# A two-level Strassen MLP: weight sums in place, input sums spread over the first block, sums written in PSUM

## The chip, the cores and the metric

The kernel runs on one core of one Trainium2 chip. The metric is the device time of one execution in microseconds; lower is better. Traces are hardware profiles of one execution.

## The reference

```python
x = attention(q, k, v)          # local band + pooled, (2, 8, 576, 64) -> x of 1152 tokens x 512
h = x @ w_in;  g = where(h > 0, h, exp(min(h, 0)) - 1);  x = g @ w_out      # first MLP, d_ff 2048
p = domain_probs / domain_probs.sum(-1)                                   # second MLP: 4 experts
for e in range(4):
    h = maximum(x @ w1[e], 0)                  # 512 -> 1024
    out += p[:, e:e+1] * (h @ w2[e])           # 1024 -> 512
```

The whole is in float32. The change is in the second MLP alone.

## The kernel before, in words

**Precision.** Each fp32 operand is kept as a high part (a ScalarE copy that rounds to fp32r) and a low part (the rest, by a subtraction), and each product is three matmul passes: high x high, low x high, high x low (`mm3`, line 237; `PASSES`).

**Blocks.** The second MLP has 8 blocks (`sbs`): 4 experts by 2 halves of 512 hidden columns. A block multiplies the input (512 x 1152, feature by token) by a 512 x 512 piece of `w1`, takes the relu into `hs` as high and low parts, and multiplies that by 512 rows of `w2` in nine tiles of 128 tokens (`l2e`, four quarters each, psZ), which VectorE scales by the probability and adds into `oacc`.

**Strassen.** The first product uses a 2 x 2 Winograd form, seven products instead of eight. Block 0 (`quad`, four times: `pair` of token quarters by `j`) uses one level: ScalarE copies the first product out of PSUM, VectorE adds the next ones to running sums c1, u2, u3, c22 in `cA` or `cB`; each of four results gets its relu high part (`hi`, ScalarE) and low part (`lo`, VectorE). Blocks 1 to 7 use two levels for three of the seven products (parts 0, 1, 3; `inner`, psA, psB, psC) and one level for the other four (`ready`, psE; `last`, psF and psG). The inner level needs sums of the inputs, which `fold(p)` makes once for all blocks: per part two VectorE sums of 576 columns (high + low), four subtractions of 288, then four high parts on ScalarE (`cp`, line 1034) and four low parts, the first on VectorE and three on GpSimd (line 1134). They go to `xq`, the fourth over an input that block 0 no longer reads (`xin`). Before the change the three folds run one after another when the four quads are issued, with three tile quarters after each.

**Weights of the next block** (`w1_two`). F loads 512 x 512 floats into a slot of the pool `s8` (eight slots of 8 KB a partition; a slot goes back by `done`). On GpSimd, T makes the sums for the inner parts, and S(j) four weight sums for the other products into a buffer `st`. H and HS write high parts on ScalarE, L and LS low parts on GpSimd. F2, H2, L2 do the same for `w2` without sums. An inner part holds a slot as `wq`, the weight sums of one j one as `ws`, the second weights two as `wr`.

**Order.** The program order of every engine is written out by the generators: `weave` takes one step of two generators in turn by a pattern; a step adds its length (0.4 per inner product, 0.8 per product, 0.68 per tile quarter) to a plan clock, and before each step `step` runs every entry of `due` whose time has come. An entry that takes a slot (F, H of the first half, HS, F2, H2) holds up those behind it until a slot is free. `plan` (line 1277) enters the weight steps for the next block relative to its start. An engine works through its own queue in this order and waits there for what an instruction needs. A block starts with `last`, woven with the tiles; the inner products come from plan time 20.0, the first of `ready` at 35.9, and a block is 45.7 long. In the first block the quads end at 27.8.

**PSUM** has eight banks, which `bank` hands out in order of their return (`psb_.done`).

Of the kernel before, what the change touches and what calls it, by code (L numbers as in the profile page):

```python
# [151 lines left out]
def attn_moe_kernel(  # L152
# [12 lines left out]
    nc = tc.nc  # L165
# [778 lines left out]
    def w1_two(n, st_pool):  # L944
# [9 lines left out]
        def F():  # L954
            raw.append(s8.tile([P, KD, SB], F32, name="raw1", uses=7))
            nc.sync.dma_start(raw[0], w1[e, :, c:c + SB].rearrange("(k p) f -> p k f", p=P))
# [4 lines left out]
        def sums(st, a11, a12, a21, a22):  # L961
            tt(out=st[0], in0=a21, in1=a22, op=add)
            tt(out=st[1], in0=st[0], in1=a11, op=sub)
            tt(out=st[2], in0=a11, in1=a21, op=sub)
            tt(out=st[3], in0=a12, in1=st[1], op=sub)
            s8.done(raw[0])
# [35 lines left out]
        def S(j):  # L1002
            sts[j] = st = st_pool[0].tile([P, 4, 2, P], F32, tag="st", name="st")
            x = view()[:, :, :, j]
            sums([st[:, o] for o in range(4)], x[:, 0, :, 0], x[:, 1, :, 0], x[:, 0, :, 1], x[:, 1, :, 1])

        def HS(j):
            mine["s", j] = s8.tile([P, 4, 2, 2, P], F32R, name="ws", uses=2)
            nc.scalar.activation(mine["s", j][:, :, 0], sts[j], AF.Copy)  # L1009

        def LS(j):
            w = mine["s", j]
            tt(out=w[:, :, 1], in0=sts[j], in1=w[:, :, 0].bitcast(F32), op=sub)  # L1013
# [3 lines left out]
    with ExitStack() as ph2:  # L1017
# [30 lines left out]

        def quad(n, j, pair):
# [3 lines left out]
            u = (cA, cB)[j]  # L1053
            c1, u2, u3, c22 = (u[:, i] for i in range(4))
            t = 2 * pair

            def prod(w, x):
                return product(bank("psH", uses=0)[:, :HB], w, x)

            cp(c1, prod(wa[:, 0], xb_[:, 0]))  # L1060
            yield 0.8
            add(u2, c1, prod(ws[:, 1], xt[:, 1]))
            yield 0.8
            add(u3, u2, prod(ws[:, 2], xt[:, 2]))
            yield 0.8
            p5 = prod(ws[:, 0], xt[:, 0])
            add(c22, u3, p5)
            add(u2, u2, p5)
            hi(dest(j, 1, t + 1), c22)
            yield 0.8  # L1070
            add(c1, c1, prod(wa[:, 1], xb_[:, 1]))
            lo(dest(j, 1, t + 1), c22)
            hi(dest(j, 0, t), c1)
            yield 0.8
            add(u3, u3, prod(wa[:, 2], xt[:, 3]))
            lo(dest(j, 0, t), c1)
            hi(dest(j, 1, t), u3)
            yield 0.8
            add(u2, u2, prod(ws[:, 3], xb_[:, 2]))
            lo(dest(j, 1, t), u3)  # L1080
            hi(dest(j, 0, t + 1), u2)
            lo(dest(j, 0, t + 1), u2)
            s8.done(wa)
            s8.done(ws)
            yield 0.8
# [33 lines left out]
        def fold(p):  # L1119

            buf = cB if p == 1 else cC
            f = buf.rearrange("p (a k) b -> p a k b", a=2)
            for pair in range(2):
                x = (xbo, xbo, None, xto)[p][pair][:, p]
                nc.vector.tensor_tensor(  # L1125
                    out=f[:, pair], in0=x[:, 0].bitcast(F32), in1=x[:, 1].bitcast(F32), op=add_
                )
            f11, f21, f12, f22 = (f[:, a, k] for a in range(2) for k in range(2))
            for o, x, y in ((f11, f12, f11), (f12, f22, f12), (f22, f22, f11), (f21, f21, f22)):
                nc.vector.tensor_tensor(out=o, in0=x, in1=y, op=sub)  # L1130
            for k, t in ((0, f11), (1, f22), (2, f12), (3, f21)):
                h, l = xin(p, k)
                cp(h, t)
                (nc.gpsimd if k else nc.vector).tensor_tensor(out=l, in0=t, in1=h.bitcast(F32), op=sub)

# [38 lines left out]

        def ready(n):
# [3 lines left out]
            for pair in range(2):  # L1179
                for j in range(2):  # L1180
                    q_ = 2 * j + pair
                    e[q_] = bank("psE")
                    ps = product(e[q_][:, :HB], wm[n][0]["s", j][:, 1], xto[pair][:, 1])
                    add(cC[:, q_], cC[:, q_], ps)
                    yield 0.8
            for pair in range(2):
                for j in range(2):
                    q_ = 2 * j + pair
                    ps = product(e[q_][:, :HB], wm[n][0]["s", j][:, 0], xto[pair][:, 0], False)
# [3 lines left out]

        late = []

        def flush(k=0):

            while len(late) > k:
                d, c, ps = late.pop(0)
                lo(d, c)  # L1200
                if ps is not None:
                    psb_.done(ps)

        def last(n, pair):
# [10 lines left out]
            for j in range(2):  # L1215
# [3 lines left out]
                ps = product(f[:, :HB], w[:, 3], xbo[pair][:, 2])  # L1219
# [71 lines left out]
        for n in range(4):  # L1291
# [70 lines left out]
```

## Time and profile before

| | |
|---|---|
| median of 3 runs | 692.0 us (690.98 to 701.45) |
| the profiled execution | 692.68 us, its span 690.9 us |
| TensorE busy, mean granted clock | 652.3 us (94%), 0.98 |
| VectorE, ScalarE, GpSimd busy | 473.6, 302.7, 323.8 us |
| HBM | 43.55 MB read, 2.36 MB written |

The span is from the first to the last instruction. The first MLP's products end at about 289 us of the span, the four quads at 318.8, block 1 begins at 362.5, block 2 at 405.7, and the last tile ends the span. [...] PE is TensorE, PEld its weight loads, DVE VectorE, ACT ScalarE, POOL GpSimd, SP the queue that issues all DMAs. "idle before <-releaser" names what ended an engine's wait. Line 240 is the one line of all matmuls, 1031 that of VectorE's sums, 1034 that of ScalarE's copies, 1037 and 1040 relu high and low parts.

### The profile page before, as it was taken

The numbers are of one execution on the slowest core, as the hardware profiler recorded it, in microseconds if no ns is written. First come the engines' busy times: TensorE is split into PE (matmuls) and PEld (weight loads), VectorE is DVE, ScalarE is ACT, GpSimd is POOL, SyncE is SP. The second block draws the span as 40 slices with busy tenths as digits, with TensorE's granted clock in tenths as the row PEclk, the third lists the DMA queues.
The fourth block names the chain that finished last, engine by engine and source line by source line (L and its number), as shares of the span: only waits on it lengthen the run. The fifth ranks groups of instructions, "written<-read, shape, count | busy, mean of one in ns | idle before, by whom it ended". The sixth has DMA issues, their size and how long they took to land.

```text
span 690.9 us, 12309 instructions
## 1 busy us (share of the span) xinstructions
PE 652.3 (94%) x4774; PEld 596.5 (86%) x4774; DVE 473.6 (69%) x976; ACT 302.7 (44%) x820; POOL 323.8 (47%) x304
## 2 busy tenths in 40 slices
PE   8999899989999999999399998998998998998997
PEld 5789789989999999998388987987987987988986
DVE  4899999645678874899757565565565575565652
ACT  4899587435664656443224323223234142233110
POOL 5533322303233537368755847637538458366000
PEclk8999999998999999999799999999999999999999
DMA  9998630051131300100031112101101101110012
GB/s 240 199 213 177 155 89 4 2 184 62 62 122 62 123 1 1 60 3 0 1 122 33 33 58 61 62 1 62 62 0 62 62 1 60 62 62 1 0 46 91
DMA packets 40735, 46.68 MB, mean 68 GB/s; under 512 B 23014, under 2 KB 23014, under 8 KB 40678
## 3 DMA queue, kind: packets, MB, share of 16 engines
q1 hardware_dynamic: 40678, 45.91, 23.8%
q8 instruction: 37, 0.61, 0.4%
q14 instruction: 20, 0.16, 0.1%
HBM read 43.55 MB, written 2.36 MB: 66 GB/s over the span
## 4 chain that ended last, share of the span: by engine, by line
PE 73%; DVE 11%; POOL 6%; ACT 4%; DMA 3%; issue 2%; SPq 0%; ACTq 0%; DVEq 0%
PE psZ L240 24%; PE psH L240 14%; PE psY L240 11%; PE psE L240 6%; PE psA L240 5%; POOL wq L998 4%; PE psB L240 2%; PE psG L240 2%; PE psF L240 2%; PE psS L582 1%; DMA raw<-in_k_dram 1%; DMA raw<-in_moe_w_in_dram 1%; DVE c L1125 1%; DVE w L308 1%; DVE c L1130 1%
## 5 line engine op out<-in xcount | busy, mean ns | idle before, releaser
L240 PE MATMUL psZ<-wr,h 128*128 128x512 f32 x864 | 226.6, 395 | 0.0
L240 PEld LDWEIGHTS psZ<-wr,h 128*128 128x128 f32 x864 | 154.7, 189 | 23.2
L240 PE MATMUL psH<-x,w 128*128 128x288 f32 x768 | 111.1, 301 | 7.5 <-DVE gf L811 4.1
L240 PEld LDWEIGHTS psH<-x,w 128*128 128x128 f32 x768 | 105.9, 192 | 9.3 <-DVE gf L811 4.5
L240 PE MATMUL psY<-g,w 128*128 128x288 f32 x768 | 106.4, 296 | 0.1
L240 PEld LDWEIGHTS psY<-g,w 128*128 128x128 f32 x768 | 103.5, 189 | 0.6 <-DVE g L823 0.3
L1103 DVE SCALAR_TENSOR_TENSOR oacc<-psZ,pn,oacc 128x512 f32<-128x512 f32 x63 | 47.2, 749 | 44.4 <-PE psZ L240 44.4
L1037 ACT ACTIVATE h<-psF 128x288 fp32r<-128x288 f32 x28 | 11.6, 413 | 116.0 <-DVE psF L1031 116.0
L823 POOL TENSOR_TENSOR g<-gf,g 128x288 fp32r<-128x288 f32 x25 | 22.0, 882 | 86.0 <-ACT g L818 84.9
L998 POOL TENSOR_TENSOR wq<-raw,wq 128x512 fp32r<-128x512 f32 x21 | 27.5, 1310 | 50.9 <-ACT wq L994 50.9
L240 PEld LDWEIGHTS psE<-xt,ws 128*128 128x128 f32 x336 | 48.2, 188 | 3.0
L1031 DVE TENSOR_TENSOR c<-psE,c 128x288 f32<-128x288 f32 x56 | 25.6, 458 | 35.9 <-PE psE L240 35.6
L240 PE MATMUL psE<-xt,ws 128*128 128x288 f32 x336 | 50.0, 295 | 0.0
L400 POOL TENSOR_TENSOR wr<-raw,wr 128x1024 fp32r<-128x1024 f32 x16 | 38.4, 2403 | 20.5 <-ACT wr L395 20.5
L1040 DVE SCALAR_TENSOR_TENSOR h<-c,h 128x288 fp32r<-128x288 f32 x72 | 45.3, 631 | 0.1
L1037 ACT ACTIVATE h<-c 128x288 fp32r<-128x288 f32 x72 | 30.1, 438 | 26.5 <-DVE c L1031 26.5
L240 PE MATMUL psA<-xq,wq 128*128 128x288 f32 x126 | 22.7, 308 | 20.0 <-ACT c L1034 20.0
L1031 DVE TENSOR_TENSOR c<-psA,c 128x288 f32<-128x288 f32 x63 | 26.9, 456 | 21.2 <-PE psA L240 21.1
L240 PEld LDWEIGHTS psA<-xq,wq 128*128 128x128 f32 x126 | 20.1, 196 | 24.6 <-ACT c L1034 22.6
L1013 POOL TENSOR_TENSOR ws<-st,ws 128x1024 fp32r<-128x1024 f32 x14 | 33.6, 2400 | 15.9 <-ACT ws L1009 15.9
L818 ACT ACTIVATE g<-gf 128x288 fp32r<-128x288 f32 x64 | 27.3, 440 | 30.9 <-DVE gf L811 24.7
L998 POOL TENSOR_TENSOR wq<-st,wq 128x512 fp32r<-128x512 f32 x21 | 29.7, 1414 | 23.2 <-ACT wq L994 23.2
(158 smaller groups left out, 1231.8 us busy)
## 6 DMA issues: line engine op xcount, KB each, us to landing
raw<-in_moe_w_dram SPq DMA_DIRECT2D x16, 1024.0 KB, 5.2
raw<-in_moe_w_in_dram SPq DMA_DIRECT2D x8, 1024.0 KB, 8.0
raw<-in_moe_w_out_dram SPq DMA_DIRECT2D x8, 1024.0 KB, 5.7
vb<-in_v_dram SPq DMA_DIRECT2D x16, 160.0 KB, 8.0
vraw<-in_v_dram SPq DMA_DIRECT2D x4, 576.0 KB
out_dram<-oacc SPq DMA_DIRECT2D x9, 256.0 KB, 2.0
raw<-in_k_dram SPq DMA_DIRECT2D x2, 576.0 KB, 8.9
raw<-in_q_dram SPq DMA_DIRECT2D x2, 576.0 KB
```

Source lines behind the costliest of these rows:

```text
L240: nc.tensor.matmul(ps, wt[a], xt[b], start=first and n == 0, stop=last and n == 2, skip_group_check=more)
L308: ENG[eng].tensor_tensor(out=t[:, 1, r], in0=up.bitcast(F32), in1=t[:, 0, r].bitcast(F32), op=ALU.subtract)
L400: nc.gpsimd.tensor_tensor(out=t[:, 1], in0=raw[0][:, 2 * j:2 * j + 2], in1=t[:, 0].bitcast(F32), op=ALU.subtract)
L582: nc.tensor.matmul(ps[par * QB:(par + 1) * QB, hp, :n], self.qkT[r, 0, hp, i * QB:(i + 1) * QB], self.qkT[r, 1, hp, lo:hi], start=False, s ...
L818: nc.scalar.activation(g[:, 0], ps1["gf", s, t, f], AF.Copy)
L823: ENG[eng].tensor_tensor(out=g[:, 1], in0=gf, in1=g[:, 0].bitcast(F32), op=ALU.subtract)
L998: tt(out=lo, in0=x, in1=hi.bitcast(F32), op=sub)
L1013: tt(out=w[:, :, 1], in0=sts[j], in1=w[:, :, 0].bitcast(F32), op=sub)
L1031: nc.vector.tensor_tensor(out=o, in0=y, in1=x, op=add_)
L1037: nc.scalar.activation(d[0], c, AF.Relu)
L1040: nc.vector.scalar_tensor_tensor(out=d[1], in0=c, scalar=0.0, in1=d[0].bitcast(F32), op0=ALU.max, op1=sub)
L1103: nc.vector.scalar_tensor_tensor(out=a, in0=ps, scalar=sc, in1=a, op0=ALU.mult, op1=ALU.add)
```

## The change

- S(j) works in the loaded block itself (GpSimd, the same four operations), so the order of the sums is by place (`wsum`), HS and LS read the block, and the block is released after LS(1) instead of S(1).
- In block 0 the last four sums of a quad are written into the product's own bank, which then stays held until its low part (`late`, `flush`, now ahead of `quad`). In `last` one more sum goes to a bank (psD) instead of `cA`. Quads use `cA` only.
- `fold` is a generator; its ten steps are entered in `due` between plan times 4 and 28.3, where the quads run. Fold 0 keeps its fourth difference in the fourth quarter of `cA`.
- The plans: in the first block H, L and S come earlier, HS and LS somewhat earlier or later; in the later blocks H of parts 1 and 3 and S(0), S(1) directly after them, HS and LS later (24.5 and 25.5 for 20 and 27.7). F2, H2, L2 and F keep their times there.
- After the quads four tile quarters are issued at once, and the weave patterns of block 1's products are those of the later blocks.

```diff
         def F():
-            raw.append(s8.tile([P, KD, SB], F32, name="raw1", uses=7))
+            raw.append(s8.tile([P, KD, SB], F32, name="raw1", uses=5))
...
@@ -1000,17 +999,21 @@
                 s8.done(raw[0])

         def S(j):
-            sts[j] = st = st_pool[0].tile([P, 4, 2, P], F32, tag="st", name="st")
             x = view()[:, :, :, j]
-            sums([st[:, o] for o in range(4)], x[:, 0, :, 0], x[:, 1, :, 0], x[:, 0, :, 1], x[:, 1, :, 1])
+            f0, f1 = [[x[:, h, :, i] for h in range(2)] for i in range(2)]
+            for o, a, b, op in (
+                (f1[1], f1[0], f1[1], add), (f1[0], f0[0], f1[0], sub), (f0[0], f1[1], f0[0], sub), (f0[1], f0[1], f0[0], sub)
+            ):
+                tt(out=o, in0=a, in1=b, op=op)

         def HS(j):
-            mine["s", j] = s8.tile([P, 4, 2, 2, P], F32R, name="ws", uses=2)
-            nc.scalar.activation(mine["s", j][:, :, 0], sts[j], AF.Copy)
+            mine["s", j] = w = s8.tile([P, 2, KD, 2 * P], F32R, name="ws", uses=2)
+            nc.scalar.activation(w[:, 0], raw[0][:, :, 2 * j * P:2 * (j + 1) * P], AF.Copy)

         def LS(j):
             w = mine["s", j]
-            tt(out=w[:, :, 1], in0=sts[j], in1=w[:, :, 0].bitcast(F32), op=sub)
+            tt(out=w[:, 1], in0=raw[0][:, :, 2 * j * P:2 * (j + 1) * P], in1=w[:, 0].bitcast(F32), op=sub)
+            s8.done(raw[0])

         return dict(F=F, T=T, H=H, L=L, S=S, HS=HS, LS=LS)
...
-            u = (cA, cB)[j]
-            c1, u2, u3, c22 = (u[:, i] for i in range(4))
+            c1, u2, u3 = (cA[:, i] for i in range(3))
             t = 2 * pair
...
-                return product(bank("psH", uses=0)[:, :HB], w, x)
+                b = bank("psH")
+                return b, product(b[:, :HB], w, x)
+
+            b, ps = prod(wa[:, 0], xb_[:, 0])
+            cp(c1, ps)
+            psb_.done(b)
             yield 0.8
-            add(u2, c1, prod(ws[:, 1], xt[:, 1]))
+            b, ps = prod(ws[:, 1], xt[:, 1])
+            add(u2, c1, ps)
+            psb_.done(b)
...
+            for w, x, y, i, k in (
+                (ws[:, 0], xt[:, 0], u3, 1, 1), (wa[:, 1], xb_[:, 1], c1, 0, 0),
+                (wa[:, 2], xt[:, 3], u3, 1, 0), (ws[:, 3], xb_[:, 2], u2, 0, 1),
+            ):
+                b, ps = prod(w, x)
+                flush()
+                if i and k:
+                    add(u2, u2, ps)
+                add(ps, y, ps)
+                d = dest(j, i, t + k)
+                hi(d, ps)
+                late.append((d, ps, b))
+                if k and not i:
+                    flush()
+                    s8.done(wa)
+                    s8.done(ws)
+                yield 0.8
...
-            buf = cB if p == 1 else cC
-            f = buf.rearrange("p (a k) b -> p a k b", a=2)
+            f = (cB if p == 1 else cC).rearrange("p (a k) b -> p a k b", a=2)
+            f11, f21, f12, f22 = (f[:, a, k] for a in range(2) for k in range(2))
+            t4 = f21 if p else cA[:, 3]
+            tt = nc.vector.tensor_tensor
             for pair in range(2):
-                x = (xbo, xbo, None, xto)[p][pair][:, p]
-                nc.vector.tensor_tensor(
-                    out=f[:, pair], in0=x[:, 0].bitcast(F32), in1=x[:, 1].bitcast(F32), op=add_
-                )
-            f11, f21, f12, f22 = (f[:, a, k] for a in range(2) for k in range(2))
-            for o, x, y in ((f11, f12, f11), (f12, f22, f12), (f22, f22, f11), (f21, f21, f22)):
-                nc.vector.tensor_tensor(out=o, in0=x, in1=y, op=sub)
-            for k, t in ((0, f11), (1, f22), (2, f12), (3, f21)):
+                x = (xbo, xbo, None, xto)[p][pair][:, p].bitcast(F32)
+                tt(out=f[:, pair], in0=x[:, 0], in1=x[:, 1], op=add_)
+                yield
+            for o, a, b in ((f11, f12, f11), (f12, f22, f12), (f22, f22, f11), (t4, f21, f22)):
+                tt(out=o, in0=a, in1=b, op=sub)
+                yield
+            for k, t in ((0, f11), (1, f22), (2, f12), (3, t4)):
                 h, l = xin(p, k)
                 cp(h, t)
                 (nc.gpsimd if k else nc.vector).tensor_tensor(out=l, in0=t, in1=h.bitcast(F32), op=sub)
+                yield

         def inner(n, p):

...
+        def wsum(n, j, o):
+            h, i = ((1, 1), (0, 0), (0, 1), (1, 0))[o]
+            return wm[n][0]["s", j][:, :, 2 * h:2 * h + 2, i * P:(i + 1) * P]
...
-                add(cA[:, q_], cA[:, q_], ps)
-                out_(j, 1, 1, cA[:, q_])
+                d = bank("psD")
+                add(d[:, :HB], cA[:, q_], ps)
+                out_(j, 1, 1, d[:, :HB], d)
...
-            (14.1, 1, "L", 0, 1), (15, 1, "T", 3), (22.5, 1, "H", 1, 0), (22.6, 1, "L", 1, 0), (23, 1, "H", 1, 1),
-            (23.1, 1, "L", 1, 1), (25, 1, "H", 3, 0), (25.1, 1, "L", 3, 0), (25.5, 1, "H", 3, 1), (25.6, 1, "L", 3, 1),
-            (27.5, 1, "S", 0), (32, 1, "HS", 0), (32.1, 1, "LS", 0), (33, 1, "S", 1), (36.5, 1, "HS", 1),
-            (36.6, 1, "LS", 1), (40, 1, "F2"), (45, 1, "H2", 0), (45.1, 1, "L2", 0), (49, 1, "H2", 1), (49.1, 1, "L2", 1),
-            (49.2, 2, "F"),
+            (14.1, 1, "L", 0, 1), (15, 1, "T", 3), (17, 1, "H", 1, 0), (17.1, 1, "L", 1, 0), (18, 1, "H", 3, 0),
+            (18.1, 1, "L", 3, 0), (19, 1, "H", 1, 1), (19.1, 1, "L", 1, 1), (20, 1, "H", 3, 1), (20.1, 1, "L", 3, 1),
+            (22, 1, "S", 0), (22.1, 1, "S", 1), (35, 1, "HS", 0), (35.1, 1, "LS", 0), (36, 1, "HS", 1), (36.1, 1, "LS", 1),
+            (38.5, 1, "F2"), (44, 1, "H2", 0), (44.1, 1, "L2", 0), (47.5, 1, "H2", 1), (47.6, 1, "L2", 1), (47.7, 2, "F"),
         )
+        for p, at in (
+            (0, (4, 5, 6.4, 7.2, 8, 8.8, 11, 11.2, 11.4, 28.1)), (1, (10, 11, 12, 13, 14, 15, 16, 16.2, 16.4, 28.2)),
+            (3, (18.5, 19.5, 20.5, 21.5, 23, 24, 24.8, 25, 25.2, 28.3)),
+        ):
+            due += [(t, False, lambda g=g: next(g)) for g in [fold(p)] for t in at]
+        due.sort(key=lambda x: x[0])
...
-                        (4.6, m, "L", 0, 1), (5, m, "T", 3), (11.6, m, "H", 1, 0), (11.7, m, "L", 1, 0), (12, m, "H", 1, 1),
-                        (12.1, m, "L", 1, 1), (13.5, m, "H", 3, 0), (13.6, m, "L", 3, 0), (14, m, "H", 3, 1),
-                        (14.1, m, "L", 3, 1), (16, m, "S", 0), (20, m, "HS", 0), (20.1, m, "LS", 0), (24, m, "S", 1),
-                        (27.5, m, "F2"), (27.7, m, "HS", 1), (27.8, m, "LS", 1), (33.5, m, "H2", 0), (33.6, m, "L2", 0),
-                        (36.2, m, "H2", 1), (36.3, m, "L2", 1), (36.4, m + 1, "F"),
+                        (4.6, m, "L", 0, 1), (5, m, "T", 3), (11.6, m, "H", 1, 0), (11.7, m, "L", 1, 0),
+                        (11.8, m, "H", 3, 0), (11.9, m, "L", 3, 0), (12, m, "H", 1, 1), (12.1, m, "L", 1, 1),
+                        (12.5, m, "H", 3, 1), (12.6, m, "L", 3, 1), (12.7, m, "S", 0), (12.8, m, "S", 1),
+                        (24.5, m, "HS", 0), (24.6, m, "LS", 0), (25.5, m, "HS", 1), (25.6, m, "LS", 1), (27.5, m, "F2"),
+                        (33.5, m, "H2", 0), (33.6, m, "L2", 0), (36.2, m, "H2", 1), (36.3, m, "L2", 1), (36.4, m + 1, "F"),
                     )
                 weave(last(n, 0), tiles(n - 1, (6, 7, 8) if n > 1 else (7, 8)), "mgmgmgmgmgmg")
                 weave(last(n, 1), tiles(n, (0, 1)), "mgmgmgmgmgmg")
@@ -1323,10 +1341,8 @@
                 weave(pre, tiles(n, (2, 3, 4, 5)), "mmmgmmgmggmg" "mmmmgmmgmmgmmgmmgmmg" "mmgmmgmmgmgmg")
             else:
                 first = tiles(0, (2, 3, 4, 5, 6))
-                for p in CH:
-                    fold(p)
-                    weave(iter(()), islice(first, 3), "")
-                weave(pre, first, "mmmgmmgmgm" "mmmmgmmgmmgmmgmm" "mmgmmgmmgmm")
+                weave(iter(()), islice(first, 4), "")
+                weave(pre, first, "mmmgmmgmggmg" "mmmmgmmgmmgmmgmmgmmg" "mmgmmgmmgmgmg")
         while due:
             due.pop(0)[2]()
```

## Rows read from the trace of the kernel before

**Rows 1.** The page, busy time of each engine (share of the span, instructions).

```profile
PE 652.3 (94%) x4774; PEld 596.5 (86%) x4774; DVE 473.6 (69%) x976; ACT 302.7 (44%) x820; POOL 323.8 (47%) x304
```

**Rows 2.** Waits of TensorE: engine, line <- what ended it: us, times, longest.

```profile
PE psA L240 <- ACT c L1034: 20.0, 6, 10.8
...
PE psB L240 <- DVE xq L1134: 0.8, 1, 0.8
...
PE psB L240 <- ACT xq L1034: 0.5, 1, 0.5
```

**Rows 3.** Timeline of TensorE, block 2: start, length, idle before <- releaser.

```profile
427.06 0.84 PE L240 MATMUL psZ<-wr,h 128*128 128x512 f32 x3
429.75 0.66 PE L240 MATMUL psA<-xq,wq 128*128 128x288 f32 x3 [1.84 <-ACT c L1034]
```

**Rows 4.** Timeline of ScalarE in the same stretch.

```profile
428.34 1.06 ACT L1009 ACTIVATE ws<-st 128x1024 fp32r<-128x1024 f32 x1 [4.43 <-POOL st L965]
429.30 0.39 ACT L1034 ACTIVATE c<-psA 128x288 f32<-128x288 f32 x1
```

**Rows 5.** Timeline of GpSimd in the same stretch.

```profile
425.16 0.95 POOL L962 TENSOR_TENSOR st<-raw 128x256 f32<-128x256 f32 x1
...
427.59 0.72 POOL L965 TENSOR_TENSOR st<-raw,st 128x256 f32<-128x256 f32 x1
```

**Rows 6.** Windows, block 3: length; PE, PEld, DVE, ACT, POOL busy; clock, DMA, GB/s.

```profile
478.00:480.00 2.00, 2.00 (x11) 1.81 (x12) 0.75 (x2) 0.51 (x2) 1.96 (x1) 0.83 0.03 8
480.00:482.00 2.00, 2.00 (x8) 1.63 (x7) 0.46 (x1) 0.00 (x0) 1.88 (x3) 0.50 0.00 0
482.00:484.00 2.00, 2.00 (x10) 1.72 (x9) 0.75 (x1) 0.61 (x2) 0.95 (x2) 0.82 0.00 0
```

**Rows 7.** Timeline of TensorE at the end of block 0.

```profile
327.97 0.86 PE L240 MATMUL psZ<-wr,h 128*128 128x512 f32 x3
339.60 1.09 PE L240 MATMUL psA<-xq,wq 128*128 128x288 f32 x3 [10.78 <-ACT c L1034]
340.49 0.92 PE L240 MATMUL psB<-xbo,wq 128*128 128x288 f32 x3
...
361.76 0.86 PE L240 MATMUL psZ<-wr,h 128*128 128x512 f32 x3
```

**Rows 8.** Windows around the end of that wait.

```profile
339.60:341.00 1.40, 1.40 (x6) 1.40 (x7) 0.44 (x1) 0.46 (x2) 1.40 (x2) 0.50 0.00 0
341.00:343.00 2.00, 2.00 (x8) 1.71 (x8) 0.46 (x1) 0.20 (x1) 1.92 (x2) 0.56 0.05 12
```

**Rows 9.** The page, groups: line, engine, operation | busy, mean ns.

```profile
L1037 ACT ACTIVATE h<-psF 128x288 fp32r<-128x288 f32 x28 | 11.6, 413 | 116.0 <-DVE psF L1031 116.0
...
L1013 POOL TENSOR_TENSOR ws<-st,ws 128x1024 fp32r<-128x1024 f32 x14 | 33.6, 2400 | 15.9 <-ACT ws L1009 15.9
```

**Rows 10.** Durations (least/median/largest, ns) by line, 285 to 345 us.

```profile
L1040 DVE SCALAR_TENSOR_TENSOR h<-c,h x16: 443/784/1321, 298.4 to 321.1; 128x288 fp32r<-128x288 f32 x16
...
L1125 DVE TENSOR_TENSOR c<-xbo x4: 1287/1319/1359, 322.0 to 328.5; 128x576 f32<-128x576 f32 x4
...
L1125 DVE TENSOR_TENSOR c<-xt x2: 748/1048/1347, 333.2 to 333.9; 128x576 f32<-128x576 f32 x2
...
L1130 DVE TENSOR_TENSOR c<-c x12: 457/458/930, 324.5 to 337.2; 128x288 f32<-128x288 f32 x12
...
L998 POOL TENSOR_TENSOR wq<-raw,wq x3: 1299/1300/1301, 306.5 to 318.1; 128x512 fp32r<-128x512 f32 x3
...
L1134 POOL TENSOR_TENSOR xq<-c,xq x6: 787/964/1362, 327.0 to 338.6; 128x288 fp32r<-128x288 f32 x6
```

**Rows 11.** Groups of VectorE by line, 340 to 691 us.

```profile
L1040 DVE SCALAR_TENSOR_TENSOR h<-psF,h 128x288 fp32r<-128x288 f32 x28 | 12.6, 449 | 0.0
```

**Rows 12.** Timeline of VectorE in the first quad.

```profile
298.03 0.45 DVE L1031 TENSOR_TENSOR c<-psH,c 128x288 f32<-128x288 f32 x1
298.39 1.32 DVE L1040 SCALAR_TENSOR_TENSOR h<-c,h 128x288 fp32r<-128x288 f32 x1
```

**Rows 13.** The chain that ended last: start, length, what.

```profile
459.27 6.18 PE psZ L240 x27
```

More of the change, by code (lines that the diff above doesn't have):

```diff
@@ L965, in sums @@
             tt(out=st[3], in0=a12, in1=st[1], op=sub)
-            s8.done(raw[0])
         def block(p):
@@ L1047, in product, with flush @@
             return ps
+        late = []
+        def flush(k=0):
+            while len(late) > k:
+                d, c, ps = late.pop(0)
+                lo(d, c)
+                if ps is not None:
+                    psb_.done(ps)
         def quad(n, j, pair):
@@ L1052, in quad @@
             xb_, xt = xbo[pair], xto[pair]
-            u = (cA, cB)[j]
-            c1, u2, u3, c22 = (u[:, i] for i in range(4))
+            c1, u2, u3 = (cA[:, i] for i in range(3))
             t = 2 * pair
             def prod(w, x):
-                return product(bank("psH", uses=0)[:, :HB], w, x)
-            cp(c1, prod(wa[:, 0], xb_[:, 0]))
+                b = bank("psH")
[3 more added lines that the diff above has]
+            psb_.done(b)
             yield 0.8
-            add(u2, c1, prod(ws[:, 1], xt[:, 1]))
+            b, ps = prod(ws[:, 1], xt[:, 1])
+            add(u2, c1, ps)
+            psb_.done(b)
             yield 0.8
-            add(u3, u2, prod(ws[:, 2], xt[:, 2]))
+            b, ps = prod(ws[:, 2], xt[:, 2])
+            add(u3, u2, ps)
+            psb_.done(b)
             yield 0.8
[L1066 to L1085, printed above, removed]
+            for w, x, y, i, k in (
[15 more added lines that the diff above has]
+                yield 0.8
         def l2e(n, t):
@@ L1182, in ready @@
                     e[q_] = bank("psE")
-                    ps = product(e[q_][:, :HB], wm[n][0]["s", j][:, 1], xto[pair][:, 1])
+                    ps = product(e[q_][:, :HB], wsum(n, j, 1), xto[pair][:, 1])
                     add(cC[:, q_], cC[:, q_], ps)
@@ L1188, in ready @@
                     q_ = 2 * j + pair
-                    ps = product(e[q_][:, :HB], wm[n][0]["s", j][:, 0], xto[pair][:, 0], False)
+                    ps = product(e[q_][:, :HB], wsum(n, j, 0), xto[pair][:, 0], False)
                     add(cA[:, q_], cA[:, q_], ps)
@@ L1192, in ready @@
                     yield 0.8
[L1194 to L1202, printed above, removed]
         def last(n, pair):
@@ L1218, in last @@
                 f = bank("psF")
-                ps = product(f[:, :HB], w[:, 3], xbo[pair][:, 2])
+                ps = product(f[:, :HB], wsum(n, j, 3), xbo[pair][:, 2])
                 flush(1)
@@ L1224, in last @@
                 g = bank("psG")
-                ps = product(g[:, :HB], w[:, 2], xto[pair][:, 2])
+                ps = product(g[:, :HB], wsum(n, j, 2), xto[pair][:, 2])
                 flush(1)
-                add(cA[:, q_], cA[:, q_], ps)
-                out_(j, 1, 1, cA[:, q_])
+                d = bank("psD")
+                add(d[:, :HB], cA[:, q_], ps)
+                out_(j, 1, 1, d[:, :HB], d)
                 add(ps, cC[:, q_], ps)
```

## The prediction

> **What bounds the kernel now.** I read the busy shares first [rows 1]: TensorE is busy for 652.3 of a span of 690.9 us, and the edits keep its products (seven per quad, seven per inner group, the same eight and eight after them). So the most that can be won is TensorE's idle time and the time it runs at half clock, and the question is which idle time goes. The waits of TensorE [rows 2] answer that: one kind, product groups in psA held up by a ScalarE copy of line 1034, is 20.0 us in 6 waits, one of them 10.8; two small waits of psB, 0.8 and 0.5, stand beside the long one. The other waits of that list are shorter or lie ahead of the second MLP.
>
> The five short waits (20.0 - 10.78 = 9.2 us, 1.84 each) repeat in blocks 2 to 6. Timeline of one [rows 3, 4, 5]: a quarter of an output tile starts at 427.06, the next product only at 429.75. It reuses a bank that ScalarE must first copy out, and that copy starts at 429.30 because it stands in ScalarE's queue behind the high part of the weight sums, which starts at 428.34, when GpSimd's last sum (427.59, 0.72 long) is done. In one block the clock then fell: windows from 478 to 484 show 0.83, 0.50 and 0.82 with TensorE fully busy [rows 6]. Lost there: 2 x (0.17 + 0.50 + 0.18) = 1.7 us.
>
> The long wait is at the first block [rows 7]: after the quarter tile at 327.97 the next product starts at 339.60. VectorE is at the folds (input sums of parts 0, 1, 3 in a row), ScalarE's copy stands behind their copies. With the two small waits 12.1 us are idle, and on resuming the clock is 0.50 and 0.56 [rows 8]: 1.40 x 0.5 + 2.0 x 0.44 = 1.6 us more.
>
> **Part 1, the high parts issued later (steady blocks).** HS(0) moves from plan time 20 to 24.5. Plan time follows TensorE closely; the held-up product has plan time 21.9 and would start at 427.75 without the wait, so 24.5 (issued at the step of 25.1) is about 431.0. S(0) then follows the four low parts at 425.16 as now and takes 428.31 - 425.16 = 3.15 us [rows 5]; S(1) now follows at once and ends near 431.5. HS(0) finds its sums ready; HS(1) may wait 0.3 us. Queued behind HS(0) on ScalarE is the copy of the seventh inner product, whose reader comes much later, and nothing that TensorE needs. GpSimd's two LS, 2.40 each [rows 9], end near 436.3; the first product with them has plan time 35.9, about 441.8: 5.5 us of cover. If that cover went, TensorE would wait at psE. The raw block is held to LS(1) instead of S(1), but the fetch of the second weights (27.5) gets the slot of part 0, free at 25.1, so SP's queue and GpSimd's later L2 keep their place. H of parts 1 and 3 come closer together on ScalarE, ahead of relus; VectorE waits for those, TensorE does not. Sum: -9.2 and -1.7 for the clock.
>
> **Part 2, sums in place.** Same 8 GpSimd operations per half, same sizes; HS and LS read as many elements from the block as from the buffer. The strided 128x512 low part from raw takes no more than 1.30 [rows 10], so I cost it at nothing.
>
> **Part 3, sums in PSUM.** Four sums per quad and one per product pair later are written in the bank. Low parts from SBUF take 443 to 1321 ns, median 784 [rows 10], from PSUM 449 [rows 11]. In the first block that takes about 16 x 0.35 = 5.6 us off VectorE. [...] In the later blocks VectorE is not the bound: nothing.
>
> **Part 4, folds spread over the first block.** This is the step that decides, and I think it mostly moves the wait. VectorE is already without a pause from 298 on (0.45 an operation, 0.36 from one start to the next [rows 12]), and three folds are 6 sums of 576 columns (0.75 to 1.35 each), 12 of 288 (0.46 to 0.93) and 3 low parts [rows 10]. Walk of VectorE's queue, from 298.03, where the first quad has three adds and four low parts left. An instruction counts 0.40; the last low part of a quad waits for its own relu (0.41 [rows 9]), so 0.5; a quad is 11 x 0.40 + 0.5 = 4.9.
> Rest of quad 1, 3.3, and two sums of fold 0 at 1.3: 303.9. Quad 2: 4.9, four subtractions at 0.55, two sums of fold 1 at 1.05 and 1.3, one low part with its copy 0.9: 314.3. Quad 3: 4.9 + 2.2 + 0.9: 322.3. With the least durations this is 319.4, with the largest 325.7.
> TensorE runs at most eight banks ahead, so it is slowed to this pace from quad 2 on.
> GpSimd's queue comes next, and every step in it waits for ScalarE's copies behind quad 3's relus. From 322.3 + 0.4: low parts 1, 2 of fold 1 at 0.96, four weight low parts at 1.30, S(0) and S(1) at 3.15, two low parts of fold 3 at 0.96, low part 3 of fold 0 at 1.0 [rows 5, 10]: 1.9 + 5.2 + 6.3 + 1.9 + 1.0 = 16.3, so 339.0. That last low part reads the fourth quarter of cA, which the copy of the second inner product overwrites; the fifth inner product waits for that copy. It starts near 339.0 + 0.5 = 339.5; today it starts at 340.49 [rows 7]. With low values all along (319.4; 1.6, 5.2, 5.9, 1.6, 0.8) it is 335.4; with all at the largest (325.7; S stretched like the low parts, 3.15 x 1.36 / 0.96 = 4.4 each) it is 347.
> From there to the end of that stage today is 361.76 + 0.69 - 340.49 = 22.0 us, with 1.1 of clock loss in it. But five quarters of tiles, 6.18 / 9 = 0.69 each [rows 13], were done inside the old wait and are now behind it: 3.5. So the stage ends at 339.5 + 22.0 + 3.5 = 365.0 against 362.5 if the clock falls again (TensorE is idle nearly 7 us before), 363.9 if not; at the low end 359.8. I take +1 us for the first block: between the two ends 0 of the low walk and +2.5 of the middle, since my 0.55 and 1.3 assume GpSimd always beside VectorE. Ends: -3, and +10 with all at the largest at once, of which I keep +5 for the range.
> On the resource behind this: in the rows, SBUF-to-SBUF work of VectorE is stretched (443 to 1321) and PSUM reading is not (449) [rows 10, 11]. [...]
>
> **Sum.** The profiled execution took 692.68 (span 690.9 and 1.8 around it), the median of the runs is 692.0. 692.68 - 9.2 - 1.7 + 1.0 = 682.8; against the median 682.1. I say 682. 2% of this kernel is 13.8 us, about what a measurement tells from no change.
>
> **Rivals.**
> 1. Forecast, 0.57: steady waits go, first block about even: 678 to 688.
> 2. The first block's wait goes as well, 0.21. For it: VectorE loses 5.6 us of work there, and median small sums are undisturbed. Then up to 12.1 + 1.6 more go: 692.7 - 9.2 - 1.7 - 13.7 = 668, and with half of it 675. Against it: GpSimd's 16 us behind quad 3.
> 3. The steady wait returns elsewhere, 0.12: HS still finds GpSimd late, or HS(1) does, so only the first block changes: 688 to 692. This is also the case in which a part doesn't do what it says. Against it: 2.7 us between S(0)'s end and HS(0)'s place.
> 4. Slower, 0.10: PSUM runs out. Three banks per product pair (psF, psD, psG) instead of two are held until a low part has run; with the relus pushed behind four weight copies TensorE waits for a bank at the end of each pair. It decides when the hold grows past about three banks' time, some 3 us. At one wait of 1.2 us per pair, 14 pairs: 682.8 + 16.8 = 700.
>
> **Numbers.** The forecast's own range is 678 to 688. To leave out no more than 2 in 10 the range must take most of rival 2 and a little of 3: 672 to 688. Faster by over 2% (below 678.2) is rival 2 and the forecast's edge: 0.26. Slower by over 2% needs 706, more than rival 4's price: 0.04. The rest, 0.70.
>
> **What would show it.** Part 1 right: no wait of TensorE for line 1034 in blocks 2 to 6, blocks of 46.3 us each, a granted clock of 1.00 past 365. Wrong: a wait of psA or psE of over 1 us each block. Part 4 right: TensorE pauses in quads 2 and 3, VectorE is never idle to 330, then a wait of psB or psA of 3 to 5 us that ends with GpSimd's low part of a fold near 339; stage end near 363. Wrong: that stage ends before 357. Part 3: low parts near 450 ns in the first block. The forecast is wrong if the first block gains more than 4 us or psF, psG or psZ wait for banks.

## The result and the profile after

The changed kernel takes 684.4 us (median of 4 runs, 683.6 to 695.4), the kernel before 693.0 beside it: a ratio of 0.988, 95% interval [0.984, 0.992], so 1.2% faster. A few executions ran slower at a lower mean clock (the one of 695.4 us, 0.966 where the other three had 0.978 to 0.982, and the profiled ones of e2 and e7 below, 0.970 and 0.975, whose excess lies ahead of the stage that is compared there); the ratios leave them out. Forecast: 682, in 672 to 688, most likely within 2%. The profiled execution took 685.16 us with a span of 683.4, against 690.9: 7.5 us less, the sum of two movements. Blocks 2 to 6 gained 12.1 us, and the first block lost 4.7; the forecast had 10.9 and 1.0.

The page, busy time of each engine, answers to [rows 1]. VectorE has 12.9 us less to do, but it is TensorE that bounds the kernel, and its busy time rose by 2.3: what was won is idle time.

```profile
PE 654.6 (96%) x4774; PEld 599.1 (88%) x4774; DVE 460.7 (67%) x976; ACT 303.0 (44%) x820; POOL 318.8 (47%) x304
```

Waits of TensorE, against [rows 2] (line 1034 of before is 1037 now, 1031 is 1034, 1040 is 1043):

```profile
PE psH L240 <- DVE h L1043: 3.4, 6, 1.3
PE psA L240 <- ACT c L1037: 3.0, 1, 3.0
PE psZ L240 <- DVE oacc L1117: 2.7, 1, 2.7
PE psB L240 <- ACT c L1037: 2.3, 1, 2.3
```

The six waits of psA, 20.0 us, are one of 3.0. All four rows lie in the first block; past 367 us of the span TensorE waits for nothing.

**A steady block.** TensorE, then ScalarE, then GpSimd in block 2, the stretch of [rows 3 to 5]:

```profile
432.37 0.55 PE L240 MATMUL psA<-xq,wq 128*128 128x288 f32 x3
...
446.44 1.75 PE L240 MATMUL psE<-xt,ws 128*128 128x288 f32 x12
```

```profile
431.09 0.41 ACT L1037 ACTIVATE c<-psA 128x288 f32<-128x288 f32 x1 [2.36 <-PE psA L240]
...
432.96 0.41 ACT L1037 ACTIVATE c<-psA 128x288 f32<-128x288 f32 x1 [1.06 <-PE psA L240]
433.27 1.05 ACT L1011 ACTIVATE ws<-raw 128x1024 fp32r<-128x1024 f32 x1
```

```profile
429.58 6.34 POOL L1007 TENSOR_TENSOR raw<-raw 128x256 f32<-128x256 f32 x8
435.88 4.78 POOL L1015 TENSOR_TENSOR ws<-raw,ws 128x1024 fp32r<-128x1024 f32 x2
```

The psA product that waited 1.84 us now starts unheld: the copy that it waited for is at 431.09, ahead of the high part (433.27); before, this copy stood directly behind the high part [rows 4]. The eight sums in place take 6.34 (2 x 3.15 were counted), the LS end at 440.66, and the first psE is at 446.44: 5.8 us of cover (5.5 were counted). Windows of block 3 against [rows 6], and two steps of the chain against [rows 13]:

```profile
470.00:480.00 10.00, 10.00 (x58) 8.87 (x57) 6.52 (x15) 5.67 (x13) 9.16 (x10) 1.00 0.01 2
480.00:490.00 10.00, 10.00 (x62) 9.09 (x62) 6.04 (x13) 2.72 (x4) 7.84 (x6) 1.00 0.28 106
```

```profile
415.81 6.17 PE psZ L240 x27
461.79 6.17 PE psZ L240 x27
```

One block is 45.98 us, five times alike, with the clock at 1.00.

**The first block.** TensorE, GpSimd and ScalarE at its end, against [rows 7]:

```profile
334.52 0.85 PE L240 MATMUL psZ<-wr,h 128*128 128x512 f32 x3
338.38 0.67 PE L240 MATMUL psA<-xq,wq 128*128 128x288 f32 x3 [3.00 <-ACT c L1037]
341.32 1.09 PE L240 MATMUL psB<-xbo,wq 128*128 128x288 f32 x3 [2.27 <-ACT c L1037]
...
367.18 0.95 PE L240 MATMUL psF<-xbo,ws 128*128 128x288 f32 x6
```

```profile
332.18 6.39 POOL L1007 TENSOR_TENSOR raw<-raw 128x256 f32<-128x256 f32 x8
338.52 1.55 POOL L1151 TENSOR_TENSOR xq<-c,xq 128x288 fp32r<-128x288 f32 x2
340.03 1.54 POOL L1151 TENSOR_TENSOR xbo<-c,xbo 128x288 fp32r<-128x288 f32 x2
```

```profile
340.86 0.41 ACT L1037 ACTIVATE c<-psB 128x288 f32<-128x288 f32 x1 [2.53 <-POOL xbo L1151]
```

The predicted chain, step for step: GpSimd's sums, its low parts of the folds, the copy of psB over the same quarter of `cA`, the fifth inner product. It starts at 341.32; the walk gave 339.5. The windows, against [rows 8], show the clock at half again behind it:

```profile
341.00:343.00 2.00, 1.68 (x5) 1.55 (x6) 0.46 (x1) 1.51 (x3) 1.74 (x3) 0.50 0.00 0
343.00:345.00 2.00, 2.00 (x7) 1.71 (x6) 0.46 (x1) 0.00 (x0) 1.96 (x1) 0.50 0.00 0
345.00:347.00 2.00, 2.00 (x9) 1.65 (x8) 0.28 (x1) 0.00 (x0) 0.00 (x0) 0.70 0.04 8
```

VectorE's timeline in the first quad, against [rows 12], shows what the walk did not have: the third add at 300.42, and its low part only after a pause. (The walk had such a pause for the fourth alone.)

```profile
300.42 0.45 DVE L1034 TENSOR_TENSOR psH<-psH,c 128x288 f32<-128x288 f32 x1
301.35 0.46 DVE L1043 SCALAR_TENSOR_TENSOR h<-psH,h 128x288 fp32r<-128x288 f32 x1 [0.48 <-ACT h L1040]
```

### The profile page after: what moved, and what is told of

Its sections match the earlier page's. It is cut to its first block, busy times and chain, and to the rows that moved or that the text cites. A ratio compares the mean times of both kernels' runs of the same rounds, so it can differ in the third digit from the quotient of the medians.

```text
span 683.4 us, 12307 instructions
## 1 busy us (share of the span) xinstructions
PE 654.6 (96%) x4774; PEld 599.1 (88%) x4774; DVE 460.7 (67%) x976; ACT 303.0 (44%) x820; POOL 318.8 (47%) x304
## 4 chain that ended last, share of the span: by engine, by line
PE 81%; DVE 11%; DMA 4%; issue 2%; ACT 1%; POOL 0%; SPq 0%; DVEq 0%; ACTq 0%; POOLq 0%
PE psZ L240 28%; PE psH L240 13%; PE psY L240 11%; PE psE L240 7%; PE psA L240 5%; PE psG L240 3%; PE psF L240 3%; PE psB L240 2%; DMA raw<-in_moe_w_in_dram 2%; PE psS L582 1%; DMA raw<-in_k_dram 1%; PE psX L642 1%; PE psC L240 1%; DVE w L308 1%; DVE psH L1034 1%
## 5 line engine op out<-in xcount | busy, mean ns | idle before, releaser
L240 PE MATMUL psZ<-wr,h 128*128 128x512 f32 x864 | 229.9, 399 | 2.7 <-DVE oacc L1117 2.7
L240 PEld LDWEIGHTS psZ<-wr,h 128*128 128x128 f32 x864 | 156.5, 192 | 26.9 <-DVE oacc L1117 2.9
L1007 POOL TENSOR_TENSOR raw<-raw 128x256 f32<-128x256 f32 x56 | 41.2, 741 | 3.3
L811 DVE SCALAR_TENSOR_TENSOR gf<-m,psH 128x288 f32<-128x288 f32 x64 | 28.2, 446 | 17.7 <-ACT m L806 12.9
L997 POOL TENSOR_TENSOR wq<-st,wq 128x512 fp32r<-128x512 f32 x21 | 27.3, 1318 | 23.3 <-ACT wq L993 23.3
L395 ACT ACTIVATE wr<-raw 128x1024 fp32r<-128x1024 f32 x16 | 17.0, 1060 | 47.3 <-DMA raw<-in_moe_w_dram 23.7
L1015 POOL TENSOR_TENSOR ws<-raw,ws 128x1024 fp32r<-128x1024 f32 x14 | 33.4, 2401 | 4.0 <-issue 3.6
L802 ACT ACTIVATE m<-psH 128x288 f32<-128x288 f32 x64 | 25.4, 403 | 20.7 <-PE psH L240 16.1
```

Source lines behind the costliest of these rows:

```text
L240: nc.tensor.matmul(ps, wt[a], xt[b], start=first and n == 0, stop=last and n == 2, skip_group_check=more)
L395: nc.scalar.activation(t[:, 0], raw[0][:, 2 * j:2 * j + 2], AF.Copy)
L802: nc.scalar.activation(m, ps1["h", s, t, f][:, :HB], AF.Relu, scale=-1.0)
L811: nc.vector.scalar_tensor_tensor(out=gf, in0=m, scalar=-1.0, in1=ps[:, :HB], op0=ALU.add, op1=ALU.max)
L997: tt(out=lo, in0=x, in1=hi.bitcast(F32), op=sub)
L1007: tt(out=o, in0=a, in1=b, op=op)
```

## The experiments

A yardstick: the *stage* is the time from the first quad product to the first psF of block 1, 73.15 us before and 77.74 after. The code ahead of it is the same in all kernels, yet that part ends anywhere from 285 to 298 us in these profiles, so totals scatter by more than the effects, and stages are compared. What lies behind the stage takes 316.2 to 316.3 us in every kernel but the one before (328.4), so no edit below moved work out of the stage. Each stage is from one profile; a hint of its noise is that before and e1, which have the same code there, differ by 0.1 us. From windows of 2 us I split a stage into TensorE's idle time and the clock's loss, the sum of busy time x (1 - granted clock); both are estimates worked out from windows. The two columns are not two prices that add up: in the changed kernel's quads, where TensorE follows VectorE, the clock falls to 0.52 (312 to 314 us) and VectorE still has no wait for TensorE in its list, so there a lower clock only takes the place of idle time.

| kernel | stage, us | idle | clock's loss | time, us | ratio to before |
|---|---|---|---|---|---|
| before | 73.15 | 13.4 | 1.6 | | |
| after | 77.74 | 12.6 | 5.7 | 684.4 | 0.988 [0.984, 0.992] |
| e1_hs_two_later | 73.04 | 13.5 | 1.4 | 681.5 | 0.982 [0.977, 0.987] |
| e2_folds_in_a_row | 75.52 | 14.4 | 2.6 | 681.5 | 0.981 [0.975, 0.987] |
| e3_sums_behind_folds | 72.86 | 10.5 | 2.8 | 682.8 | 0.981 [0.972, 0.990] |
| e4_nine_quarters | 74.36 | 10.2 | 4.8 | 684.6 | 0.985 [0.973, 0.996] |
| e5_low_one_later | 73.60 | 11.4 | 3.9 | 679.9 | 0.981 [0.971, 0.991] |
| e6_row_low_later | 71.33 | 11.4 | 2.8 | 679.9 | 0.976 [0.968, 0.985] |
| e7_all_three | 70.48 | 9.0 | 3.0 | 682.4 | 0.973 [0.963, 0.983] |
| e8_fold3_later | 71.16 | 9.4 | 3.1 | 683.6 | 0.980 [0.971, 0.990] |
| e9_folds_in_gaps | 70.96 | 11.0 | 2.6 | 678.8 | 0.984 [0.978, 0.989] |
| e10_quad_alone | 75.36 | 14.3 | 2.4 | 683.9 | 0.987 [0.979, 0.994] |
| e11_inner_first | 67.28 | 7.9 | 1.4 | 675.8 | 0.976 [0.967, 0.986] |

**One high part moved, in the kernel before.**

```diff
-(16, m, "S", 0), (20, m, "HS", 0), (20.1, m, "LS", 0),
+(16, m, "S", 0), (22, m, "HS", 0), (22.1, m, "LS", 0),
```

> The kernel before with one thing changed: in the plan of the later blocks the high part HS(0) and low part LS(0) are entered at 22.0 and 22.1 instead of 20.0 and 20.1, which puts HS(0) behind the copies of the first inner products in ScalarE's queue. My theory: the place of this one instruction is the whole of the steady gain, so blocks 2 to 6 last 46.0 us instead of 48.1 to 49.7, and the time falls by 12, from 692.5 to about 680.5 (ratio 0.983), below the changed kernel. Rival: the gain of the later blocks came from sums in place or sums in PSUM, then TensorE still waits 1.84 us in each of five blocks somewhere (psA or psE) and the time stays at 690 to 693.

Measured: the waits of psA, and a step of the chain,

```profile
PE psA L240 <- ACT c L1034: 10.8, 1, 10.8
```

```profile
412.14 6.17 PE psZ L240 x27
458.12 6.17 PE psZ L240 x27
```

so 45.98 a block, exactly the changed kernel's. The whole gain of the steady blocks is this one instruction's place on ScalarE (the low part LS(0), which reads it, moves along on GpSimd). By itself it is worth more than the whole change, whose first block is 4.7 us longer. Sums in place and sums in PSUM, which this kernel lacks, give and cost these blocks nothing that shows.

**The folds in a row again, all else as changed.** `fold` runs to its end in the old loop over `CH`, three quarters after each, with the old weave patterns.

> The changed kernel with the three folds undone to the old place: one after another behind the quads, three tile quarters after each, and the old weave patterns of block 1; all else as changed. My theory: spreading the folds cost 4.7 us in the first block, so without it block 1 starts at 362.5 or earlier (low parts out of PSUM free VectorE by up to 3 us: 359.5) instead of 367.2, and the time is 677 to 680 (ratio to the kernel before 0.978 to 0.982). Rival: the first block was lost to the weight sums issued earlier on GpSimd or to the held banks, which are still there: block 1 starts near 367 and the time is 684.

Not so: 75.52. With no fold between them, the changed quads still cost more than the old ones. VectorE's timeline of two sums says why, and its waits add up to 7.2 us in 15:

```profile
317.53 0.46 DVE L1034 TENSOR_TENSOR psH<-psH,c 128x288 f32<-128x288 f32 x1
318.47 0.46 DVE L1043 SCALAR_TENSOR_TENSOR h<-psH,h 128x288 fp32r<-128x288 f32 x1 [0.48 <-ACT h L1040]
318.84 0.46 DVE L1034 TENSOR_TENSOR psH<-psH,c 128x288 f32<-128x288 f32 x1
319.77 0.46 DVE L1043 SCALAR_TENSOR_TENSOR h<-psH,h 128x288 fp32r<-128x288 f32 x1 [0.48 <-ACT h L1040]
```

`flush()` stands ahead of the next add: each low part comes directly behind the add whose relu it needs. A quad takes 6.72 us of VectorE (316.04 to 322.76), where the walk had 4.9.

**GpSimd's sums behind the folds' low parts.**

```diff
-(22, 1, "S", 0), (22.1, 1, "S", 1),
+(28.4, 1, "S", 0), (28.5, 1, "S", 1),
```

> The changed kernel with S(0) and S(1) of the first block entered at 28.4 and 28.5, behind the last low parts of the folds in GpSimd's queue, instead of 22.0 and 22.1. My theory: GpSimd's queue sets the fifth inner product (341.32); with the 6.4 us of weight sums out of its way the low part of fold 0 comes right after its ScalarE copy, the fifth product starts near 338.9 and block 1 2.4 us earlier: 682 (ratio to the changed kernel 0.9965). Rival: VectorE's lag alone sets the end of the first block and GpSimd only follows: gain under 0.5, 684.

The wait of psB is gone, that of psA is 1.84 instead of 3.00:

```profile
344.52 0.67 PE L240 MATMUL psA<-xq,wq 128*128 128x288 f32 x3 [1.84 <-ACT c L1037]
345.03 0.56 PE L240 MATMUL psB<-xbo,wq 128*128 128x288 f32 x3
```

The stage is 4.9 us shorter. The fifth product comes 49.3 us after the first quad product (345.03 - 295.74) instead of 51.9 (341.32 - 289.44), 2.6 earlier where 2.4 were expected. The other 2.3 come behind it, where the granted clock was 0.50 for four us (341 to 345) and in this run is 1.00:

```profile
345.00:347.00 2.00, 2.00 (x14) 1.78 (x13) 0.74 (x2) 0.41 (x1) 1.92 (x4) 1.00 0.00 0
```

**Nine quarters ahead of the wait, as before.**

```diff
-weave(iter(()), islice(first, 4), "")
+weave(iter(()), islice(first, 9), "")
```

(and the old patterns).

> The changed kernel with nine tile quarters behind the quads instead of four, and the old weave patterns of block 1 (as many quarters in all). My theory: TensorE is idle for 5 us before the fifth inner product in any case, so five quarters of 0.69 done inside that wait come off behind it: block 1 starts near 363.8 and the time falls 3.4 to 681. Rival: the extra products hold banks or VectorE's output scaling pushes the folds back: no gain, 684.

Stage 3.4 us shorter, as expected, and all of it behind the fifth product, which stays 51.9 us after the first quad product. The time alone, with its wide interval, would not have shown it.

**Low parts one sum later in the quads.**

```diff
-                flush()
+                flush(1)
```

> The changed kernel with one word changed in the quads: behind each of the last four products one low part stays pending (flush(1) instead of flush()), so that a low part no longer stands directly behind the relu it needs. My theory: the quads' low parts wait 0.48 us each for their relu (3.5 us in 8 waits of VectorE here, 7.2 in 15 with the folds in a row, none in the kernel before), which is the term that I mis-sized; without them the first block is 2 to 3.5 us shorter (74.2 to 75.7 from the first quad product to block 1 instead of 77.7), 681 to 682. Rival: the waits are covered by the folds' own work and GpSimd's queue sets the end: under 0.7 us, 684.

Stage 73.60, 4.1 less, more than expected; no wait of VectorE for a relu is left in its list, and the wait of psB grew, as its copy waits longer for GpSimd:

```profile
PE psB L240 <- ACT c L1037: 3.8, 1, 3.8
```

Of this, 4.0 us are there when quad 3's last low part ends: 30.3 us after the first quad product instead of 34.3. The five waits up to there account for 2.1 of them, fold sums that are shorter here for most of the rest (9.3 us instead of 10.8 for the twelve of quads 1 to 3). From then on the chain is the same: in both kernels 9.1 us pass from GpSimd's first sum in place to the fifth product. Banks are held longer here than in the changed kernel, so the holding of banks is not what cost the time.

**Both: folds in a row, low parts one later.** The two edits above.

> Folds in a row as in the run with that name, and one low part left pending in the quads. My theory: VectorE's 7.2 us of waits go and it follows TensorE again, which ends the quads about 3 us before VectorE there; the folds start 2.5 to 3 us earlier, the stage from the first quad product to block 1 is 72.6 (75.5 without, 73.15 in the kernel before), 678 to 679. Rival: SBUF sums of the folds are what is long, and the stage stays at 75.

71.33, 4.2 below e2: the same step once more, without the folds between. It is also 1.7 below e1: without the pauses, sums in PSUM would have shortened the stage (the rest of the change moves it by 0.2, e2 against e10). TensorE still has its one long wait of psA, 9.8.

**Sums behind the folds, nine quarters and low parts one later, together.**

> The changed kernel with the weight sums behind the folds' low parts on GpSimd, nine tile quarters behind the quads, and one low part left pending. My theory: the three gains have different places (GpSimd's queue, TensorE's idle time, VectorE's waits) and mostly add: 72.9 with the first alone, 2 to 3.4 less by the quarters, 2 to 3 less by the low parts: stage 67 to 69, time 675 to 677, faster than both kernels. Rival: one resource, VectorE's work of 56 us with its contention, sets the stage whatever the order: 71 to 73, 679 to 681.

70.48, between the two. Three edits that gave 4.9, 3.4 and 4.1 alone give 7.3: they shorten in part the same waits.

**Fold 3 later.** From e7, its ten steps at plan times 22.3 to 28.3 (18.5 before).

> As the one before, with fold 3 entered from 22.3 to 27.5 instead of 18.5 to 25.2, so that the scaling of tile 1 no longer stands behind fold 3's sums on VectorE. My theory: the 2.7 us for which TensorE waits for tile 1's bank behind the quads go, and fold 3 is not needed before the second group of inner products: stage 1 to 2 us shorter than the one before. Rival: the same work lies behind quad 4 then, and the copies of the first inner product wait for it: no shorter, or up to 2 us longer.

71.16: the wait of psZ for `oacc` (2.7) is gone and psA waits 4.9 in 2 instead. The rival was right.

**Folds in gaps.** From e7, fold 0 at 16.9 to 21.1, fold 1 at 28.2 to 31.2, fold 3 at 32.3 to 35.5, the sums S back at 22.

> The changed kernel with one low part left pending in the quads, nine tile quarters behind them, and the folds put where VectorE has room and no later than needed: fold 0 beside the two tiles between quads 3 and 4, fold 1 beside the nine quarters, fold 3 beside the first group of inner products. My theory: what is left of the wait (9.8 us of idle TensorE with the folds in a row, 10 in small waits with them spread over the quads) comes from fold work standing ahead of something that TensorE needs; in this order the products of the quads are never behind a fold and the first inner group needs fold 0 alone, so the first stage is 60 to 65 us instead of 70.5 to 77.7 and the time 667 to 673 (ratio to the kernel before 0.962 to 0.972). Rival: VectorE's total work in the stage, 56 us, plus GpSimd's contention is the floor already, stage 69 to 71, time 677 to 680.

A miss: 70.96, the rival's figure (though e11 below shows that this is no floor). A quad now takes VectorE 4.90 us (299.96 to 304.86), but TensorE waits behind the copies of the folds, which stand in ScalarE's queue ahead of those of the inner products:

```profile
PE psA L240 <- ACT c L1037: 8.4, 2, 5.1
```

**The changed quads alone, in the kernel e1.** `quad` and `flush` from the changed kernel, nothing else (line numbers as in the kernel before).

> The kernel before with HS two later (as in the first experiment) and, of the rest of the change, the quads alone: last four sums in the product's bank, the low part flushed ahead of the next sum. My theory: each of these low parts stands directly behind the relu it waits for, VectorE waits 7 us in about 15 waits for ScalarE that it did not have before, and the first stage grows from 73.0 by 2 to 3 us to 75 to 76. Rival: low parts out of PSUM spare VectorE more (5.6 us by my prediction) than they wait, and the stage shrinks to 68 to 71.

75.36, 2.3 above e1, and VectorE's waits are those of e2:

```profile
DVE h L1040 <- ACT h L1037: 7.2, 15, 0.5
```

So the quads as changed cost 2.3 us by themselves.

**The first inner group ahead of the folds' copies.** From e9:

```diff
-            (1, (28.2, 28.9, 29.5, 29.6, 30.2, 30.3, 30.9, 31, 31.1, 31.2)),
-            (3, (32.3, 33, 33.6, 33.7, 34.1, 34.5, 35.2, 35.3, 35.4, 35.5)),
+            (1, (28.5, 29.2, 30, 30.4, 30.8, 31.2, 33.9, 34, 34.1, 34.2)),
+            (3, (34.5, 35, 36, 36.7, 37.4, 38.1, 40, 40.1, 40.2, 40.3)),
...
-                weave(iter(()), islice(first, 9), "")
-                weave(pre, first, "mmmgmmgmgm" "mmmmgmmgmmgmmgmm" "mmgmmgmmgmm")
+                weave(iter(()), islice(first, 5), "")
+                weave(pre, first, "mmmgmmgmgm" "gggggggg" "mmmmgmmmmmmmmmm" "mmgmmgmmgmm")
```

and S at 28.3, 28.4.

> The kernel of e9_folds_in_gaps with folds 1 and 3 put behind the copies of the first block's first inner group in ScalarE's order, the sums S back between plan units 28 and 29, and eight quarters of quad products, held back for it, given to TensorE while VectorE does these folds. Theory (the copies of an inner group stand in ScalarE's queue behind fold copies that wait for VectorE, and TensorE has nothing else to do meanwhile): the inner group no longer waits, and the stage from the first quad product to the first psF of block 1 is 62 to 66 us, against 70.96 in e9; time 668 to 673 us. Rival (VectorE's fold work of this stage ends at the same time wherever the copies stand, and sets the end): 69 to 71 us, time 677 to 680 us.

67.28, just above the theory's range and well below the rival's; at 675.8 us this had the lowest median of all (by the ratio it cannot be told from e6 and e7). The copies no longer hold TensorE up, and most of what is left is VectorE itself:

```profile
PE psA L240 <- DVE c L1034: 4.5, 2, 4.1
```

Its timeline and GpSimd's show the four small subtractions of a fold taking 1.4 us each in the mean, while GpSimd works through low parts:

```profile
333.66 5.62 DVE L1146 TENSOR_TENSOR c<-c 128x288 f32<-128x288 f32 x4
```

```profile
333.63 1.78 POOL L1151 TENSOR_TENSOR xq<-c,xq 128x288 fp32r<-128x288 f32 x2
335.37 1.02 POOL L1151 TENSOR_TENSOR xbo<-c,xbo 128x288 fp32r<-128x288 f32 x1
336.36 5.18 POOL L1015 TENSOR_TENSOR ws<-raw,ws 128x1024 fp32r<-128x1024 f32 x2
```

## Why the prediction was right, and where it was not

**Part 1, right, its size a little low.** The steady wait was the high part's place in ScalarE's queue: e1 shows it by moving that instruction and the low part behind it alone. Forecast 9.2 and 1.7 for the clock, measured 12.1: the 27-product steps of before are 48.09 apart without a fall of the clock and 49.67 with one, now 45.98, so 5 x 2.11 = 10.6 for the waits and 1.6 for the clock. A wait costs more than the 1.84 that its row shows: from the quarter at 427.06 in [rows 3] the next product would have followed 0.69 later, at 427.75, and came at 429.75, 2.0 later. HS(0) ran at 433.27, 22.9 after the block's start and not 25.3 as I placed it; its sums were ready, so that changed nothing.

**Part 2, right.** 6.34 us for the eight sums in place, and the same 45.98 with and without them (e1). The weight low parts, which I had counted at 1.30, took 1.48 in the first block (line 997 below): small, but more than nothing.

**Part 3, the step that failed.** The duration was right: low parts from PSUM take 456 ns in the median.

```profile
L1043 DVE SCALAR_TENSOR_TENSOR h<-psH,h x16: 443/456/460, 298.1 to 337.1; 128x288 fp32r<-128x288 f32 x16
```

But I let only the last low part of a quad wait for its relu ("so 0.5; a quad is 4.9"). The diff issues each of the four directly behind its own add, and each can stand idle for 0.48 us. In the changed kernel fold steps fill half of them: 8 such waits, 3.5 us, are left, of which four stand before the last low part of a quad, as I had counted. A quad's own VectorE time is 6.72 to 6.78 (e2, e10), not 4.9, which is what e9 measured with the low parts one sum later. Alone the changed quads cost 2.3 us (e10), where I had counted on relief; with this one argument changed the stage loses 4.1 (e5), 4.2 with the folds in a row (e6). The 5.6 us off VectorE were won (the 16 low parts took 13.4 us before and take 7.2) and, without folds between, more than given back as pauses (7.2 in e10).

**Part 4, the mechanism right, the choice on the low side.** What the walk named was seen: TensorE slowed to VectorE's pace in the quads, GpSimd's queue behind quad 3, the fourth quarter of `cA`, the wait of psB; e3 and e4 show by removal the sums on that path and the price of five quarters behind it (3.4; 3.5 were counted). The walk's middle gave a stage end at 365.0, and I took 363.5, between it and the low walk (which ends at 359.8, 2.7 us ahead of before, and not at the 0 that I wrote), since I thought its 0.55 and 1.3 for fold sums assumed too much of GpSimd. They did not. Durations by line between 285 and 345 us (least/median/largest, ns), against [rows 10]:

```profile
L1143 DVE TENSOR_TENSOR c<-xbo x4: 1177/1320/1720, 298.9 to 313.0; 128x576 f32<-128x576 f32 x4
...
L1146 DVE TENSOR_TENSOR c<-c x12: 441/618/1432, 304.5 to 330.5; 128x288 f32<-128x288 f32 x12
...
L997 POOL TENSOR_TENSOR wq<-raw,wq x3: 1284/1475/1479, 309.2 to 327.8; 128x512 fp32r<-128x512 f32 x3
```

The trace of before had 458 for the small sums because its folds ran in a row, while GpSimd paused between their low parts (nine of the twelve have no GpSimd instruction beside them, and take 457 to 459); among GpSimd's weight steps they cost more (five of the twelve have none beside them, and the twelve take 9.0 us instead of 6.9). The actual end is 367.18, 2.2 behind the walk: 1.8 by the fifth product, of which 1.5 were there when quad 3's last low part ended (323.8, the walk had 322.3), and 0.4 behind it. Nearly all of the 1.5 arose in quad 3: fold 1's four subtractions took 3.3 us there, two of them beside GpSimd, where the walk had 2.2, and the low part with its copy 1.3 for 0.9. Up to quad 2 the walk was met within 0.2 us, although the pauses that it lacked come to 0.7 there. The earlier falls of the clock, inside the quads (0.52 and 0.63 from 312 to 316 us, 0.54 and 0.61 from 329 to 333), cost nothing that shows: VectorE, which sets the pace there, has no wait for TensorE in its list between 284 and 340 us. By stages: folds spread and four quarters together cost 2.2 (after against e2), of which the quarters are 3.4, so that the spread as such won 1.2.

In sum the first block lost 3.7 us more than I said (4.7 for 1.0), and the steady blocks won 1.2 more (12.1 for 10.9). The two misses have opposite signs, so it is in part luck that the profiled execution came within 2.4 us of the forecast (685.2 for 682.8).

**The rivals.** The first block's wait did not go, but could have gone in part: with the low parts one sum later, and folds and quarters placed by ScalarE's queue, e11 has a stage 5.9 us shorter than before, half of that rival's 12.1. No wait of HS or psE came in place of the old one. Rival 4's bank wait did come, but in the quads, 3.4 us in 6 waits of psH for a low part, and not at the product pairs, where I had put it: psF, psD and psG never wait. One of my signs of being wrong came true: psZ waits once, 2.7 us, for a bank that VectorE has yet to scale out, behind fold 3's sums. And one sign of Part 4 being right did not: VectorE is idle before 330, 2.1 us in five waits for relus and 0.8 for a fold's copy.

**Open.** Why three edits overlap to 7.3 was read from the waits that remain and not taken apart further; nor was a place of the folds tried in which GpSimd is idle and TensorE has work.

## What to carry to other kernels

In a queue that runs in order, look at what stands directly behind an instruction that must wait for another engine, and at what directly precedes a reader: one ScalarE copy issued two steps later was worth 2.1 us a block, and one low part issued directly behind its producer cost up to 0.48 us each time, though its own duration fell (784 to 456 ns in the median). Price a moved operation with the neighbours that it will have, not with the median of where it stood. Compare stages, and not totals, when the part ahead of the change varies by more than the effect.

## What the runs showed of the hardware

VectorE's small sums within SBUF (128x288, fp32), twelve in the first block of a kernel, took 441 to 459 ns where no GpSimd instruction ran beside them (nine of the kernel before, five of the changed one) and 614 to 1432 ns where one did (the other ten). Their median was 458 before, 618 after, 883 in e9 and 914 in e11, where the longest took 2534. The changed kernel's 16 low parts read from PSUM took 443 to 460 ns, with a GpSimd instruction beside them (ten) or without (six).
